# Attention scores of the first four stages read keys in place, and scale factors are finished on all partitions by one product each

## The chip, the cores and the metric

One core of a Trainium2 chip runs the whole program. The metric is the device time of one execution in microseconds (us); lower is better. Engines: PE is the matrix engine (PEld its weight loads), DVE the vector engine, ACT the activation engine, POOL the general engine, SP the queue that issues the DMAs.

## The reference, cut to what matters

```python
# q, k, v: (4, 8, 768, 64) float32; w_in (512, 2048), w_out (2048, 512) float64
k_sum = k.reshape(B, H, 24, 32, D).max(axis=3)       # one key for each block of 32
v_sum = v.reshape(B, H, 24, 32, D).mean(axis=3)
scores_l = scale * q @ k^T, kept where |i - j| < 16   # a band of 31 keys
scores_s = scale * q @ k_sum^T + log(32)              # 24 block keys
a = softmax(concat[scores_l, scores_s])               # minus row max; / (sum + 1e-9)
x = (a @ concat[v, v_sum]) with heads side by side    # (3072, 512)
h = x @ w_in;  out = (h * sigmoid(h)) @ w_out
```

## The kernel before, in words

The 3072 tokens are cut into 24 stages of 128 tokens (six for each of the four batches) and the feed-forward part into 12 chunks of 256 tokens, two stages each. A stage scores its 128 queries against a window of 158 keys and against the 24 block keys, so a score tile is 128x182. The first chunks need stages 0 to 3 before any feed-forward product can run.

Stages 0 to 5 (batch 0) multiply in float32; the first `NPL` = 4 stages are "plain" all through. Stages of later batches use pairs of float16, for which q, k and v are divided by power-of-two scales found from the data. A stage's steps and their lines in the kernel before:

- `job_k` (L365, L366): keys of a batch are loaded as four tiles (one for each pair of heads, 128x768) and DVE takes the maximum of each block into `km`. For batch 0 these tiles lie in space (`wt`) that holds weights later, and are free after the maximum.
- `job_qk` (L480, L492 to L497): for batch 0, `qkT` brings each pair of heads' 128 queries and 158 window keys in one DMA of 128x286, sixteen of them for stages 0 to 3; the 24 block keys are copied behind them by ACT or POOL (L214, L216).
- `job_mean` (L506, L523 to L528): six float32 products with `blocks` give the block means of v in bank 6, and DVE the largest |v|.
- `job_a` (L591 to L637): one score step on PE holds two pairs of heads, four products 64x128 by 64x182, the two heads of a pair on the upper and lower 64 rows of the array. DVE adds the mask and takes the maximum (L599), ACT the exponential (L602). In plain stages PE turns the result (L611, L613), and ACT or DVE copies it out.
- `job_c`, `job_x` (L657, L691, L695 to L697): PE multiplies by v and spreads 1/sum, DVE scales (L695), ACT rounds to `xh`, POOL or DVE takes the rest `xl`.
- `job_w` (L716 to L744): each of 16 weight tiles (1 MB) is loaded, changed from float64 bits to float32 by ACT and DVE, and scaled by a maximum over all partitions (L740).
- `job_f` (L801, L810): the two feed-forward products. ffn1 of a chunk and a tile f is two runs of 12 products, each 128x256; ffn2 is 12 products of 128x512.
- scales: `job_scale` (q and k), `v_scale` and `job_wo` (weights out). A column of 128 maxima is turned by PE into one row (L384, L425, L760), DVE works on that one partition (for q and k L388 to L394, seven short steps), PE spreads the results with a product with `ones` (L398, L437, L771), and DVE copies them out (L400, L438, L772).

The order on every engine is worked out when the program is built: a planner (`Plan`) takes the jobs with listed costs and priorities, assigns each to an engine, and writes each engine's queue. The priorities come from the table `TUNE`. Where it sees PE waiting at the start, it puts in idle products (L324, 128x256 bf16, result unused) to keep the clock up; it stops with them when the first feed-forward products stand.

Of the kernel before, what the change touches and what calls it, by code (L numbers as in the profile page):

```python
# [21 lines left out]
P = 128  # L22
# [185 lines left out]
def local_attn_ffn(ctx: ExitStack, tc: tile.TileContext, qkT, qF, qD, kF, kD, v, vR, w, out):  # L208
# [41 lines left out]
    ones = const.tile([1, P], F32, name="ones")  # L250
    nc.vector.memset(ones, 1.0)
# [15 lines left out]
    sc3 = const.tile([1, 4], F32, name="sc3")  # L267
# [29 lines left out]
    qc = const.tile([1, 10], F32, name="qc")  # L297
# [5 lines left out]
    sc2 = const.tile([1, 4], F32, name="sc2")  # L303
# [53 lines left out]

    def job_k(b, prio):
# [12 lines left out]
    def job_scale(b, prio):  # L371
# [9 lines left out]

        def tr(e, k=k):
# [3 lines left out]
        plan.op({"pe": 220}, tr, r=["qm_q", "qm_k"], w=[("bank", k)], prio=prio, cols=256)  # L386
        steps = (
            lambda e, k=k: nc.vector.tensor_reduce(out=qc[:, 0:2], in_=bank[k][:1, :2 * P].rearrange("o (a p) -> o a p", a=2), axis=AX.X, op=ALU.max),  # L388
# [3 lines left out]
            lambda e: nc.vector.reciprocal(out=qc[:, 6:8], in_=qc[:, 4:6]),  # L392
            lambda e: nc.vector.scalar_tensor_tensor(out=qc[:, 8:9], in0=qc[:, 4:5], scalar=-ISQ, in1=qc[:, 5:6], op0=ALU.mult, op1=ALU.mult),
            lambda e: nc.vector.scalar_tensor_tensor(out=qc[:, 9:10], in0=qc[:, 6:7], scalar=math.log(BLK) / ISQ, in1=qc[:, 7:8], op0=ALU.mult, op1=ALU.mult))  # L394
        for i, step in enumerate(steps):
            plan.op({"dve": 330 if i == 0 else 70}, step, r=[("bank", k)] if i == 0 else [], w=["qc"], prio=prio)
        k = sbank()
        plan.op({"pe": 110}, lambda e, k=k: nc.tensor.matmul(out=bank[k][:, :4], lhsT=ones, rhs=qc[:, 6:10], start=True, stop=True), r=["qc"], w=[("bank", k)], prio=prio, cols=1)  # L398
        qs = qsc_t[b % 2]
        plan.op({"dve": 67}, lambda e, k=k: nc.vector.tensor_copy(out=qs, in_=bank[k][:, :4]), r=[("bank", k)], w=[("qsc", b % 2)], prio=prio)  # L400
# [22 lines left out]
    def v_scale(b, prio):  # L423
        k = sbank()
        plan.op({"pe": 110}, lambda e, k=k: nc.tensor.transpose(out=bank[k][:1, :P], in_=am_t[:, 7:8], identity=ident), r=["am4"], w=[("bank", k)], prio=prio, cols=128)  # L425

        steps = (
            lambda e, k=k: nc.vector.tensor_reduce(out=sc2[:, 0:1], in_=bank[k][:1, :P], axis=AX.X, op=ALU.max),
# [3 lines left out]
            lambda e: nc.vector.reciprocal(out=sc2[:, 2:3], in_=sc2[:, 1:2]),  # L432
            lambda e: nc.vector.tensor_scalar(out=sc2[:, 3:4], in0=sc2[:, 1:2], scalar1=0.25, scalar2=None, op0=ALU.mult))
        for i, step in enumerate(steps):
            plan.op({"dve": 198 if i == 0 else 70}, step, r=[("bank", k)] if i == 0 else [], w=["sc2"], prio=prio)
        k = sbank()
# [540 lines left out]
```

## Time and profile before

| | |
|---|---|
| median of 3 runs | 631.01 us (630.73 to 631.74) |
| the profiled execution | 631.93 us, of which span 630.1 us |
| PE busy | 614.5 us (98%), 5008 products |
| DVE, ACT, POOL busy | 470.2, 397.2, 186.0 us |
| moved by DMA | 94.77 MB, mean 150 GB/s |

A row of the timeline gives start, duration, engine, line, operation, and in brackets how long the engine was idle before it and what ended that. Products are pipelined: a product's duration is its latency, and what a run of them costs is read from the distance between starts.

### The profile page before, as it was taken

Reading aid. Unit: us, or ns where it says so; the run is one execution under the profiler, and the core shown is the slowest. Engines: PE = TensorE matmul, PEld = TensorE weight load, DVE = VectorE, ACT = ScalarE, POOL = GpSimd, SP = SyncE. Lnnn points to the kernel's source line nnn. Section 1 sums busy time; section 2 is a strip of 40 time slices with the busy share of each in tenths; the row PEclk is TensorE's granted clock in tenths of the full one; section 3 lists DMA queues with packets and bytes.
Section 4 is the critical chain, followed back from the end, with each engine's and each line's share of the span. In section 5 each row is a group of like instructions: output and inputs, shape, how many; then the busy total and the mean of one; then the engine's idle time right before and its main releaser. Section 6 shows DMA issues by size and latency. Waiting matters only on the chain. (4 is left out here: it accounts for less than half of the span.)

```text
span 630.1 us, 13616 instructions
## 1 busy us (share of the span) xinstructions
PE 614.5 (98%) x5008; PEld 422.3 (67%) x5008; DVE 470.2 (75%) x1317; ACT 397.2 (63%) x860; POOL 186.0 (30%) x213
## 2 busy tenths in 40 slices
PE   7999999999999998999999998999999999999997
PEld 3877666666666765767767765766767767767674
DVE  7899877999797857898888864699888884562322
ACT  2899998764787666566676564565775673452322
POOL 3010531322734523325443253133343323110000
PEclk8999999999999999999999999999999999999999
DMA  9994755346574994454764774457566740220000
GB/s 300 363 377 196 277 171 167 85 135 182 152 173 121 205 232 151 121 152 111 155 176 111 205 203 125 122 147 158 165 153 122 208 101 14 59 39 14 34 1 33
DMA packets 92566, 94.77 MB, mean 150 GB/s; under 512 B 70460, under 2 KB 73532, under 8 KB 90452
## 3 DMA queue, kind: packets, MB, share of 16 engines
q1 hardware_dynamic: 92500, 93.91, 54.1%
q8 instruction: 39, 0.64, 0.5%
q14 instruction: 27, 0.22, 0.1%
HBM read 69.41 MB, written 6.29 MB: 120 GB/s over the span
## 5 line engine op out<-in xcount | busy, mean ns | idle before, releaser
L810 PE MATMUL bank<-wt,g 128*128 128x512 f16 (+1 forms) x1120 | 276.9, 392 | 4.7 <-POOL g L232 3.2
L801 PE MATMUL bank<-xh,wt 128*128 128x256 f16 x1536 | 269.8, 273 | 1.0 <-DVE raw L835 0.9
L801 PEld LDWEIGHTS <-wt 128*128 128x128 f16 x2304 | 224.3, 98 | 46.5 <-issue 6.5
L801 PE MATMUL bank<-xl,wt 128*128 128x256 f16 x768 | 209.3, 273 | 1.4 <-DVE xl L229 1.4
L810 PEld LDWEIGHTS <-g 128*128 128x128 f16 x1056 | 100.6, 98 | 107.5 <-POOL g L232 6.7
L816 DVE SCALAR_TENSOR_TENSOR t<-t,bank 128x512 f32<-128x512 f32 x96 | 65.5, 682 | 70.5 <-ACT t L815 70.2
L232 POOL TENSOR_TENSOR g<-t,g 128x512 f16<-128x512 f32 x56 | 72.4, 1292 | 152.6 <-ACT g L820 134.4
L815 ACT ACTIVATE t<-bank,asc 128x512 f32<-128x512 f32 x96 | 65.4, 681 | 81.8 <-PE bank L801 81.7
L602 ACT ACTIVATE e<-e,mx 128x182 f32<-128x182 f32 x192 | 83.6, 437 | 21.9 <-DVE mx L599 21.2
L637 DVE SCALAR_TENSOR_TENSOR p<-e,sum,p 128x128 f16<-128x128 f32 x320 | 89.7, 343 | 3.3 <-ACT p L624 2.4
L820 ACT CAST g<-t 128x512 f16<-128x512 f32 x88 | 54.0, 614 | 34.0 <-DVE t L816 33.5
L599 DVE CUSTOM_DVE_ANT_0 e<-bank,masks,qsc 128x182 f32<-128x182 f32 x144 | 52.1, 401 | 8.4 <-PE bank L594 8.1
L626 POOL TENSOR_SCALAR p<-e,sum 128x182 f16<-128x182 f32 x62 | 28.6, 470 | 99.4 <-ACT e L602 36.2
L624 ACT ACTIVATE p<-e,sum 128x182 f16<-128x182 f32 x75 | 30.3, 439 | 22.7 <-DVE sum L619 8.5
L232 POOL TENSOR_TENSOR vv<-raw,vv 128x1024 f16<-128x1024 f32 x17 | 37.5, 2206 | 14.8 <-ACT vv L214 10.9
L232 DVE TENSOR_TENSOR g<-t,g 128x512 f16<-128x512 f32 x32 | 31.1, 973 | 13.9 <-ACT g L820 12.8
L602 ACT ACTIVATION_READ_ACCUMULATOR e<-e,mx 128x1 f32 x192 | 36.0, 188 | 0.0
L497 DVE SCALAR_TENSOR_TENSOR qk<-raw,qsc,qk 64x1264 f16<-64x1264 f32 x18 | 28.9, 1608 | 5.9 <-ACT qk L496 3.8
L496 ACT ACTIVATE qk<-raw,qsc 128x1264 f16<-128x1264 f32 x18 | 24.2, 1345 | 11.7 <-DMA raw<-in_kD_dram 11.5
L593 PE MATMUL bank<-qk 128*128 128x182 f16 x144 | 27.8, 242 | 0.0
L594 PE MATMUL bank<-qk 128*128 128x182 f16 x144 | 27.8, 242 | 0.0
L670 PE MATMUL bank<-tt,vv 128*64 128x128 f16 x800 | 26.1, 220 | 0.0
(153 smaller groups left out, 632.0 us busy)
## 6 DMA issues: line engine op xcount, KB each, us to landing
wt<-in_w_dram SPq DMA_DIRECT2D x16, 1024.0 KB
raw<-in_kD_dram SPq DMA_DIRECT2D x18, 632.0 KB
raw<-in_v_dram SPq DMA_DIRECT2D x20, 512.0 KB
raw<-in_qD_dram SPq DMA_DIRECT2D x18, 512.0 KB
out_dram<-raw SPq DMA_DIRECT2D x24, 256.0 KB
raw<-in_kF_dram SPq DMA_DIRECT2D x12, 384.0 KB
raw<-in_qF_dram SPq DMA_DIRECT2D x9, 512.0 KB
raw<-in_vR_dram SPq DMA_DIRECT2D x12, 384.0 KB
```

What stands on the lines that cost most here:

```text
L232: eng[e].tensor_tensor(out=out, in0=in0, in1=in1, op=ALU.subtract)
L497: plan.op({"dve": 1450}, lambda e: nc.vector.scalar_tensor_tensor(out=kst[64:, :, :NLOC], in0=kr[64:], scalar=qs[64:, 1:2], in1=kst[64:, : ...
L599: plan.op({"dve": 258 if b == 0 else 323}, lambda e, i=i: nc.vector.tensor_tensor_reduce(out=et[:, i, :NKEY], in0=sc[:, i, :NKEY], in1=mas ...
L602: plan.op({"act": 431}, lambda e, i=i, h=h: nc.scalar.activation(out=et[:, i, :NKEY], in_=et[:, i, :NKEY], func=AF.Exp, scale=-1.0, bias=m ...
L624: nc.scalar.activation(out=out, in_=et[:, i, :NKEY], func=AF.Copy, scale=by)
L626: nc.gpsimd.tensor_scalar(out=out, in0=et[:, i, :NKEY], scalar1=by, scalar2=0.0, op0=ALU.mult, op1=ALU.add)
L637: nc.vector.scalar_tensor_tensor(out=pt[:, i, to:to + z - a], in0=et[:, i, a:z], scalar=su[:, i:i + 1], in1=pt[:, i, a:z], op0=ALU.mult, o ...
L801: nc.tensor.matmul(out=h[:, d * CH:(d + 1) * CH], lhsT=wt[f, 0][:, part, d, ct * P:(ct + 1) * P], rhs=x[:, ct, :], start=(ct == 0 and q == ...
L810: nc.tensor.matmul(out=bank[ob[u]], lhsT=a[:, d * CH + u * P:d * CH + u * P + P], rhs=b[:, d, :], start=(opens and d == 0 and q == 0), sto ...
L815: plan.op({"act": 640}, lambda e: nc.scalar.activation(out=t, in_=h, func=AF.Tanh, scale=asc_t[c // 3 % 2][:, f:f + 1]), r=[("bank", k), ( ...
L816: plan.op({"dve": 605}, lambda e: nc.vector.scalar_tensor_tensor(out=t, in0=t, scalar=1.0, in1=h, op0=ALU.add, op1=ALU.mult), r=[("bank", ...
L820: plan.op({"act": 540}, lambda e: nc.scalar.copy(out=gh, in_=t), r=[("t", j)], w=[("gh", n)], prio=at - TUNE["post"])
```

## The change

Plain stages no longer load windows of keys. Their scores read the keys from the four tiles that `job_k` loads, with zeros of 15 columns on each side (POOL, eight memsets), and the block keys from `km`: a score step has eight products (158 and 24 columns) in place of four (182). The window is contiguous (15 before to 15 after), so these stages have a mask of their own (`band`), rows of v in another order, and left operands of the block means to match (`blocks0`, `blocks1`). Only the queries are loaded, two DMAs of 128x256 for each of the four stages. The key tiles stay in use until the scores of stage 3. The 24-column copies now serve stages 4 and 5.

Scales: one float32 product of the column, spread over 128 columns, with the identity puts all 128 values on every partition. DVE does the same short steps on 128 partitions and writes the last into their place; the second product and the copy are gone. `TUNE` is changed.

```diff
@@ job_k
+            if b == 0:
+                plain_k[hp] = stg[:, :S + 2 * HALO], key
+                kf = stg[:, HALO:HALO + S]
+                for side in (stg[:, :HALO], stg[:, HALO + S:S + 2 * HALO]):
+                    nc.gpsimd.memset(side, 0.0)
@@ job_scale (v_scale and job_wo alike)
-                nc.tensor.transpose(out=bank[k][:1, j * P:(j + 1) * P], in_=qm_t[:, 3 + 5 * j:4 + 5 * j], identity=ident)
+                nc.tensor.matmul(out=bank[k][:, j * P:(j + 1) * P], lhsT=qm_t[:, 3 + 5 * j:4 + 5 * j].to_broadcast([P, P]), rhs=ident, start=True, stop=True)
...
-        plan.op({"pe": 110}, lambda e, k=k: nc.tensor.matmul(out=bank[k][:, :4], lhsT=ones, rhs=qc[:, 6:10], start=True, stop=True), ...)
-        plan.op({"dve": 67}, lambda e, k=k: nc.vector.tensor_copy(out=qs, in_=bank[k][:, :4]), ...)
@@ job_qk
+        if s < NPL:
+            qk = qk_t[s % 2].bitcast(F32)[:, :4 * P].rearrange("p (a n) -> p a n", a=4)
+            for hp in range(0, 4, 2):
+                plan.op({"dma": 460}, lambda e, hp=hp: nc.sync.dma_start(out=qk[:, hp:hp + 2], in_=q0[t, :, hp:hp + 2]), ...)
+            return
@@ job_a
-        mask = masks[:, 0 if t == 0 else (2 if t == NTILE - 1 else 1), :]
+        mask = band[:, 0 if t == 0 else 1, :] if s < NPL else masks[:, 2 if t == NTILE - 1 else 0 if t == 0 else 1, :]
...
+                        if plain:
+                            at = i * 256
+                            for rhs in (plain_k[hp][0][pr, t * P:t * P + NLOC], km_t[0][pr, hp, :]):
+                                to = at + rhs.shape[-1]
+                                nc.tensor.matmul(out=bank[k + o][:, at:to], lhsT=qk[pr, hp, :], rhs=rhs, start=True, stop=True)
+                                at = to
+                            continue
```

On PE, the first products after the idle ones. `wt_76` and `wt_77` hold v, `wt_68` and `wt_69` keys, `qk0` the first stage's queries (before: with keys). Before:

```order
L525 MATMUL bank6_205<-wt_76,blocks_105 24x512
L525 MATMUL bank6_205<-wt_77,blocks_105 24x512
...
L591 MATMUL bank2_201<-qk0_151 128x182
L591 MATMUL bank3_202<-qk0_151 128x182
...
L525 MATMUL bank6_205<-wt_71,blocks_105 24x512
```

After:

```order
L619 MATMUL bank2_224<-wt_69,qk0_174 128x158
L619 MATMUL bank2_224<-km0_182,qk0_174 128x24
L619 MATMUL bank3_225<-wt_69,qk0_174 128x158
L619 MATMUL bank3_225<-km0_182,qk0_174 128x24
...
L549 MATMUL bank6_228<-wt_76,blocks0_114 24x512
L549 MATMUL bank6_228<-wt_77,blocks1_109 24x512
```

The first score step has moved ahead of the block means of v, four of which stood before it. Up to the first feed-forward product there stood five score steps, nine turned banks (four products each), two spreads of 1/sum and 61 idle products; now there stand seven, twelve, three and 48.

On SP, the loads around the weights of tile f = 2 (`wt_68` and `wt_69`) and f = 3 (`wt_70` and `wt_71`), with what each waits for (DMAHW are the DMA queues' own). Before:

```order
L716 DMA wt_64<-in_w_dram 128x2048 [waits DMAHW2_49]
...
L716 DMA wt_66<-in_w_dram 128x2048 [waits DMAHW7_49]
L716 DMA wt_65<-in_w_dram 128x2048 [waits DMAHW0_49]
...
L716 DMA wt_68<-in_w_dram 128x2048 [waits DMAHW3_49,DVE_49]
...
L716 DMA wt_70<-in_w_dram 128x2048 [waits DMAHW6_49,DVE_49]
```

After:

```order
L753 DMA wt_67<-in_w_dram 128x2048 [waits DMAHW7_49]
...
L753 DMA wt_72<-in_w_dram 128x2048 [waits DMAHW2_49]
L753 DMA wt_73<-in_w_dram 128x2048 [waits DMAHW3_49]
...
L753 DMA wt_74<-in_w_dram 128x2048 [waits DMAHW5_49]
L753 DMA wt_68<-in_w_dram 128x2048 [waits DVE_49,DMAHW6_49,PE_49,Pool_49]
...
L753 DMA wt_70<-in_w_dram 128x2048 [waits DVE_49,DMAHW1_49,PE_49,Pool_49]
```

The loads of `wt_68` and `wt_70` have moved from fourth and fifth of the weight loads to eighth and ninth, and wait for PE too, whose last reader of those tiles is stage 3's scores.

On PE, the scale of q and k for batch 1, near 127 us of the profile before: the second product stands between two halves of an ffn2. Before:

```order
L810 MATMUL bank4_203<-wt_79,g2_198 128x512
L398 MATMUL bank6_205<-qc_156,ones_85 128x4
L810 LDWEIGHTS g2_198
L810 MATMUL bank5_204<-wt_79,g2_198 128x512
...
L591 MATMUL bank6_205<-qk1_152 128x182
```

After, the only product of that scale stands inside an ffn1:

```order
L835 MATMUL bank1_223<-xh1_214,wt_78 128x256
L409 MATMUL bank6_228<-ident_80,qm_178 128x128 x2
L835 LDWEIGHTS wt_78
L835 MATMUL bank1_223<-xh1_214,wt_78 128x256
L835 LDWEIGHTS wt_78
```

The visit that waited for the seven DVE steps is gone; what is left takes the place of L384.

More of the change, by code (lines that the diff above doesn't have):

```diff
@@ L391, in job_scale @@
             lambda e: nc.vector.tensor_scalar(out=qc[:, 4:6], in0=qc[:, 2:4], scalar1=2.0 ** -14, scalar2=None, op0=ALU.mult),
-            lambda e: nc.vector.reciprocal(out=qc[:, 6:8], in_=qc[:, 4:6]),
-            lambda e: nc.vector.scalar_tensor_tensor(out=qc[:, 8:9], in0=qc[:, 4:5], scalar=-ISQ, in1=qc[:, 5:6], op0=ALU.mult, op1=ALU.mult),
-            lambda e: nc.vector.scalar_tensor_tensor(out=qc[:, 9:10], in0=qc[:, 6:7], scalar=math.log(BLK) / ISQ, in1=qc[:, 7:8], op0=ALU.mult, op1=ALU.mult))
+            lambda e: nc.vector.reciprocal(out=qs[:, 0:2], in_=qc[:, 4:6]),
+            lambda e: nc.vector.scalar_tensor_tensor(out=qs[:, 2:3], in0=qc[:, 4:5], scalar=-ISQ, in1=qc[:, 5:6], op0=ALU.mult, op1=ALU.mult),
+            lambda e: nc.vector.scalar_tensor_tensor(out=qs[:, 3:4], in0=qs[:, 0:1], scalar=math.log(BLK) / ISQ, in1=qs[:, 1:2], op0=ALU.mult, op1=ALU.mult))
         for i, step in enumerate(steps):
[L396 to L400, printed above, removed]
+            plan.op({"dve": 330 if i == 0 else 70}, step, r=[("bank", k)] if i == 0 else [], w=["qc"] + ([("qsc", b % 2)] if i > 3 else []), prio=prio)
     def job_km(b, prio):
@@ L475, in job_qk @@
         b, t = divmod(s, NTILE)
+        if s < NPL:
+            qk = qk_t[s % 2].bitcast(F32)[:, :4 * P].rearrange("p (a n) -> p a n", a=4)
+            for hp in range(0, 4, 2):
+                plan.op({"dma": 460}, lambda e, hp=hp: nc.sync.dma_start(out=qk[:, hp:hp + 2], in_=q0[t, :, hp:hp + 2]), w=[("qk", s % 2, hp + i) for i in range(2)], prio=prio + hp // 2)
+            return
         if b == 0:
@@ L524, in job_mean @@
             at = (NTILE - 1 - t) * 4
-            plan.op({"pe": 1020}, lambda e, src=src, t=t, at=at, k=k: nc.tensor.matmul(out=bank[k][:NB], lhsT=blocks[:, at:at + NB], rhs=src, start=(t == 0), stop=(t == NTILE - 1)),
+            of = blocks0 if t == 0 else (blocks1 if t < NPL else blocks)[:, at:at + NB]
+            plan.op({"pe": 1020}, lambda e, src=src, t=t, of=of, k=k: nc.tensor.matmul(out=bank[k][:NB], lhsT=of, rhs=src, start=(t == 0), stop=(t == NTILE - 1)),
                     r=key, w=[("bank", k)], prio=prio, cols=2048)
@@ L596, in job_a @@
         if b or g % 2 == 0:
-            plan.op({"pe": 330 if b else 820}, scores, r=[(x, s % 2, hp) for x in ("qk", "qkm") for hp, _ in heads(g)] + [("qkk", s % 2)], w=[("bank", k)] if b else [("bank", k), ("bank", k + 1)], prio=prio, cols=728)
+            need = [("qk", s % 2, hp) for hp, _ in heads(g)] + [("qkk", s % 2)]
+            if plain:
+                need += [(x, s % 2, hp) for x in ("qk", "qkm") for hp in range(4) if (x, s % 2, hp) not in need]
+                need += [x for hp, _ in heads(g) for x in [("km", hp)] + plain_k[hp][1]]
+            else:
+                need += [("qkm", s % 2, hp) for hp, _ in heads(g)]
+            plan.op({"pe": 330 if b else 950 if plain else 820}, scores, r=need, w=[("bank", k)] if b else [("bank", k), ("bank", k + 1)], prio=prio, cols=728)
         for i, (hp, h) in enumerate(heads(g)):
@@ L853, in job_stage @@
         if s == 0:
-            plan.op({"pool": 1}, lambda e: None, w=["mask"] + [("qkk", i) for i in range(2)], prio=-90.0)
+            plan.op({"pool": 1}, lambda e: None, w=["mask"] + [("qkk", i) for i in range(2)] + [("qkm", i, hp) for i in range(2) for hp in range(4)], prio=-90.0)
             job_k(0, -74)
@@ L904, in local_attn_ffn @@
     plan.issue()
[L907 removed]
+TUNE = dict(wo=1725.55, kap=515.89, km=254.54, w_dma=-435.28, w_dec=16.19, a0=529.03, a1=-254.77, d1=354.23, span=-231.56, post=-299.98, ffn2=-1403.83, jc0=2185.03, jc1=787.71, jx0=754.54, jx1=-298.86, vs=2845.05, qk=-522.95, k=325.28, v=1913.04, v0=-151.46, out=847.66, first=347.6)
 NUDGE = {}
[L913 removed]
+_INS = ["q0", "qkT", "qF", "qD", "kF", "kD", "v", "vR", "w"]
 def _layout(inputs):
```

77 lines of the change are left out of this document (47 added, 30 removed).

## The prediction

> **What bounds the kernel now.** I read the page first, then the time by stretches, then the timeline of the first 46 us, then the waits of PE.
>
> ```profile
> PE 614.5 (98%) x5008; PEld 422.3 (67%) x5008; DVE 470.2 (75%) x1317; ACT 397.2 (63%) x860; POOL 186.0 (30%) x213
> PEclk8999999999999999999999999999999999999999
> L324 PE MATMUL bank<-ident 128*128 128x256 bf16 x61 | 9.4, 305 | 1.4 <-POOL ident masks.py:199 1.4
> ```
>
> PE is busy for 614.5 of 630.1 us, so 15.6 us are idle, and part of the busy time is the 61 idle products. What is to be had are those, the idle time, and products that can be left out. Where they lie, in stretches (length, busy time of PE, PEld, DVE, ACT and POOL with counts, granted clock, DMA share, GB/s):
>
> ```profile
> 0.00:5.00 5.00, 3.64 (x20) 2.60 (x20) 3.56 (x20) 1.28 (x1) 3.20 (x17) 1.00 0.63 203
> 5.00:10.00 5.00, 2.81 (x5) 0.57 (x5) 4.97 (x9) 0.64 (x3) 1.78 (x5) 0.76 1.04 359
> 10.00:15.00 5.00, 5.00 (x19) 1.52 (x18) 2.77 (x11) 1.28 (x6) 0.21 (x1) 0.90 1.10 327
> 15.00:20.00 5.00, 5.00 (x41) 3.48 (x40) 3.96 (x21) 3.94 (x16) 0.00 (x0) 1.00 0.80 259
> 30.00:35.00 5.00, 4.95 (x51) 4.01 (x48) 5.00 (x13) 5.00 (x11) 2.46 (x2) 1.00 1.01 400
> 125.00:150.00 25.00, 22.74 (x185) 14.38 (x184) 24.23 (x66) 13.64 (x34) 4.82 (x7) 1.00 0.56 154
> 225.00:250.00 25.00, 22.64 (x190) 15.45 (x189) 14.62 (x31) 13.41 (x25) 7.26 (x6) 1.00 0.71 197
> 375.00:400.00 25.00, 22.99 (x193) 15.63 (x192) 12.82 (x28) 12.79 (x22) 6.39 (x4) 1.00 0.47 138
> ```
>
> Two kinds of place: the first 15 us, where PE, DVE and ACT wait for data and PE loses 3.6 us, and three spots of about 2 us where a new batch comes in. At 30 to 35 us DVE and ACT are full. The timeline shows what starts the work:
>
> ```profile
> 5.38 2.60 DVE L366 TENSOR_REDUCE km<-wt 128x24 f32<-128x768 f32 x3
> 7.29 5.29 PE L525 MATMUL bank<-wt,blocks 128*24 128x512 f32 x8 [2.19 <-DMA wt<-in_v_dram]
> 11.21 0.95 DVE L366 TENSOR_REDUCE km<-wt 128x24 f32<-128x768 f32 x1 [0.86 <-DMA wt<-in_kF_dram]
> 12.51 0.89 PE L591 MATMUL bank<-qk 64*128 64x182 f32 x8
> 13.33 0.50 PE L324 MATMUL bank<-ident 128*128 128x256 bf16 x3
> 13.54 0.35 DVE L599 CUSTOM_DVE_ANT_0 e<-bank,masks 128x182 f32<-128x182 f32 x1 [1.38 <-PE bank L591]
> 22.76 1.09 PE L691 MATMUL bank<-ident,ss 128*64 128x128 f32 x16
> 23.58 0.91 PEld L657 LDWEIGHTS bank<-wt 128*64 128x64 f32 x16
> 30.54 0.89 PE L591 MATMUL bank<-qk 64*128 64x182 f32 x8
> 31.36 3.01 PE L324 MATMUL bank<-ident 128*128 128x256 bf16 x26
> 31.76 0.68 DVE L695 TENSOR_TENSOR xr<-bank,xr 128x512 f32<-128x512 f32 x1
> 34.78 0.29 PEld L611 LDWEIGHTS bank<-ident,e 128*128 128x128 f32 x2
> 35.25 1.30 PEld L801 LDWEIGHTS <-wt 128*128 128x128 f16 x12
> ```
>
> The first mask step waits for the first score step, which stands behind four block means. The first feed-forward product starts at 35.25; the second scaling (L695) that its input needs ends at 32.44. Two costs are read here from distances: a score step is 0.82 us (30.54 to 31.36), a spread of 1/sum 0.82 (22.76 to 23.58), a turned bank 0.47 (34.78 to 35.25), an idle product 0.11 to 0.12 (3.06 us for 26).
>
> **The change part by part.**
>
> Start of the first scores. The step needs two key tiles, their maxima and the first queries, no longer four block means and a late copy. DVE's three maxima start at 5.38, 0.87 us each, right behind its setup. The change adds eight short setup steps there, about 0.6 us by the length of the ones shown (fills of 128x474: 0.45), so they come at 6.0, the second is done at 7.7. The score step then runs when the clock was halved before (0.76 in 5 to 10 us), so I double it to 1 to 2 us; the planner has put one |v| maximum ahead on DVE. First mask step at about 9.6 in place of 13.54: 3.9 us earlier. POOL's extra masks and the zero columns, fourteen steps, end before 8 by its rows of 0.1 to 0.3 us.
>
> What DVE then does up to the second scaling. Counted in the order, the changed kernel has 8 more mask steps (0.27 apart), 3 more |v| maxima, one more key maximum, one weight maximum and one xr scaling more, and two copies and the vsc copy less:
>
> ```profile
> 7.90 2.45 DVE L528 TENSOR_REDUCE am<-wt 128x1 f32<-128x512 f32 x4
> 24.98 1.20 DVE L736 TENSOR_REDUCE wm<-wt 128x1 f32<-128x1024 f32 x1
> 28.76 0.75 DVE L226 TENSOR_SCALAR xr<-bank,vsc 128x512 f32<-128x512 f32 x1 [0.57 <-PE bank L691]
> 27.50 0.63 DVE L218 COPY wt<-bank 128x512 f32<-128x512 f32 x1
> 22.12 0.14 DVE L438 COPY vsc<-bank 128x2 f32<-128x2 f32 x1
> ```
>
> 2.2 + 1.8 + 0.9 + 1.2 + 0.75 - 1.3 - 0.1 = 5.4 us. The second scaling ends at 32.4 - 3.9 + 5.4 = 33.9, 1.5 us later than before. PE's own list up to the same point, from 7.7: seven score steps, six means (0.86 each, half of 1.9 for four rows at the full clock being 0.95), twelve banks at 0.47, three spreads at 0.82, two products with v at 2.0, small ones 0.5, 27 idle ones at 0.11: 8.2 + 5.2 + 5.6 + 2.5 + 4.0 + 0.5 + 3.0 = 29.0, so 36.7, or 37.7 with the slow clock. I take the first feed-forward product at 37.2, 2.0 us later. By then PE has done more: two score steps, three banks and one spread, 1.64 + 1.41 + 0.82 = 3.9 us. Net 1.9 us gained, provided PE stays full afterwards, which the stretches after 35 us allow.
>
> A split score step. It has 16 records in place of 8. Per half of the array before: four streams of 0.15 us (0.61 in all, the loads' row below). After: four of 158/182 of that, and four short ones that cost no less than a weight load. A 128-column float32 load is 0.11 us by the spread's row (0.29 for two with a tail of 0.18). If both halves run side by side as now: 4 x 0.13 + 4 x 0.11 = 0.97, so 0.35 more. Bounds: nothing (hidden loads), or 16 loads one after another, 1.75 in place of 0.82, so 0.93 more. I take 0.35, since the row shows eight loads in 0.61. Seven of eight steps are in the list above (at 1.17 each); the last costs 0.35.
>
> ```profile
> 21.95 0.61 PEld L591 LDWEIGHTS bank<-qk 64*128 64x128 f32 x8 [0.21 <-issue]
> 21.31 0.29 PEld L437 LDWEIGHTS bank<-sc,ones 1*128 1x128 f32 x2 [0.37 <-DVE sc L433]
> 21.62 0.39 PE L324 MATMUL bank<-ident 128*128 128x256 bf16 x2
> ```
>
> [...]
>
> Scales. After 35 us ten transposes (0.11 each, one record) become products of two records (0.22 by the turned bank's two), 1.1 us more; seven second products go, 0.31 each (21.31 to 21.62), 2.2 us less: 1.1 us gained on PE, as PE is full. DVE's short steps on 128 partitions in place of one I cost at nothing: a two-element step of 128 partitions (L438) took 0.14 us, as those on one did; a maximum over 128x128 in place of 1x128 the same. Bounds: 0 to 0.1 us for each chain, off PE's path. With the second product goes PE's wait for the chain:
>
> ```profile
> 126.93 0.38 PE L398 MATMUL bank<-qc,ones 1*128 1x4 f32 x2 [0.98 <-DVE qc L394]
> 127.60 1.16 POOL L232 TENSOR_TENSOR g<-t,g 128x512 f16<-128x512 f32 x1 [3.92 <-DVE qsc L400]
> PE bank L810 <- POOL g L232: 3.2, 5, 1.0
> ```
>
> 0.98 us were lost there; behind it stood half an ffn2. I take 0.5 of it, between 0 and 0.98, because the next PE waits are for POOL's g (3.2 us in five places), which the chain does not shorten. The other waits of that kind I leave as they are: the whole order is new, and they may come out either way by about 3 us.
>
> Loads. Stages 0 to 3 bring 0.26 MB in place of 0.59 each: 1.3 MB, at 400 GB/s 3.3 us of a queue that is full in the first 45 us. I give no time for it: the weights of f = 0 and 1 come earlier, and DVE, ACT and PE, not they, end the start. Eight DMA issues fewer on SP.
>
> Sum: -1.9 + 0.35 - 1.1 - 0.5 = -3.2 us. The profiled execution took 631.93 (630.1 of span and 1.8 around it) and would take 628.7; it lies 0.9 above the median 631.01, so the median goes to 627.8.
>
> **The rivals.**
>
> More than that: the waits at the batches' borders go as well. They are 2.3, 2.4 and 2.0 us in the three stretches above; if half of them go, 624.5. For it: the chains are shorter there. Against it: most of that idle time ends with POOL's g, not a scale.
>
> No change: weights of f = 2 and 3 come late. Their tiles hold the keys until stage 3's scores, and the loads stand on SP behind that wait, with all later loads behind them. In the trace a 1 MB load takes 2.6 us at 400 GB/s, plus about 2 to start, and the steps after it (L724, L726, L736, L222, L229 by their rows 6.0, with the maximum over partitions) some 6.6:
>
> ```profile
> 28.78 1.13 ACT L222 ACTIVATE wt<-wt,ur 128x1024 f16<-128x1024 f32 x1
> 30.56 1.28 DVE L229 SCALAR_TENSOR_TENSOR wt<-wt,ur 128x1024 f16<-128x1024 f32 x1
> 31.39 1.16 ACT L724 ACTIVATE wt<-wt 128x1024 f32<-128x1024 f32 x1
> 29.43 1.22 DVE L726 SCALAR_TENSOR_TENSOR wt<-wt 128x1024 uint32<-128x1024 uint32 x1
> ```
>
> With stage 3's first scores done at 37, f = 2 could be ready at 48, and PE's list reaches it some 17 to 19 us after its first ffn1, at 55; for f = 3 there are some 6 us. If queues on the full DVE and ACT eat more than these 6 to 7 us, PE waits; 3 us of it gives 631.
>
> Slower: the split step runs its loads one after another, 1.75 us each. Seven steps before the first ffn1 then cost 4.1 us more than I took, the last 0.6: 627.8 + 4.7 = 632.5. It decides from about 1.6 us a step on.
>
> Little changes at all: DVE, not PE, sets the start, and later starts eat the gain. That gives the same 631 as the late weights.
>
> **How the numbers follow.** A measurement of this kernel can tell 0.2%, 1.3 us, from no change: faster is below 629.7, slower above 632.3. My forecast (627.8, its own range 626.0 to 629.6) 0.46; more than that (624.5) 0.17; no change (631) 0.22; slower (632.5 and above) 0.15. So faster 0.63, same 0.22, slower 0.15. The range from 624.6 to 632.3 leaves out the tails of the first and last rivals, about 0.2.
>
> **What would show it.** The first mask step near 9.6 us and the first ffn1 near 37; 16 loads of a score step in 1.0 us and not 1.7; no wait of PE on a scale's DVE steps; idle products 48; weights of f = 2 ready before PE reaches them, that is no PE wait on a weight's DVE or ACT step at 45 to 65 us. Wrong would be a first ffn1 after 40, a second half-clock stretch (each is 3.4 us by the 0.76 and 0.90 above, and costs up to 1.7), or more than 9 us of PE idle time after 100 us.

## The result, and the profile after

The change makes the kernel slower: 639.28 us (median of 4 runs, 636.7 to 640.5) against 630.9 (now median of 4 runs of the kernel before, 630.73 to 631.74), a ratio of 1.0121 with a 95% interval of 1.0082 to 1.0160. I had said 627.8, so the sign was wrong and the time off by 11.5 us. The profiled execution took 640.47, its span is 638.6.

First the page of the kernel after, then the same stretches of time as before (length, busy time of PE, PEld, DVE, ACT and POOL with counts, granted clock, DMA share, GB/s):

```profile
PE 618.1 (97%) x5054; PEld 425.6 (67%) x5054; DVE 477.6 (75%) x1310; ACT 397.2 (62%) x871; POOL 190.5 (30%) x222
```

```profile
5.00:10.00 5.00, 2.96 (x20) 1.99 (x18) 4.73 (x9) 0.00 (x0) 3.50 (x19) 0.92 1.01 368
10.00:15.00 5.00, 5.00 (x12) 1.46 (x11) 4.43 (x14) 1.83 (x8) 0.00 (x0) 0.50 1.05 393
15.00:20.00 5.00, 5.00 (x38) 2.61 (x39) 1.62 (x9) 2.40 (x8) 0.00 (x0) 0.90 0.35 82
125.00:150.00 25.00, 23.63 (x200) 15.78 (x198) 24.34 (x65) 13.97 (x34) 4.55 (x6) 1.00 0.58 149
225.00:250.00 25.00, 22.35 (x221) 15.56 (x221) 19.06 (x59) 17.57 (x47) 10.38 (x11) 1.00 0.72 184
375.00:400.00 25.00, 24.07 (x201) 16.26 (x199) 18.43 (x58) 12.85 (x32) 4.99 (x7) 1.00 0.49 111
```

The clock column now has 0.92, 0.50 and 0.90 where before had 0.76 and 0.90. In steps of 0.5 us the column falls to 0.50 and no lower in both traces (8.0 to 11.0 us before, 9.5 to 16.0 after). So the time at half clock is twice what is missing to 1: 2 x 5 x (0.08 + 0.50 + 0.10) = 6.8 us, and before 2 x 5 x (0.24 + 0.10) = 3.4 us. In the three later stretches, where PE lost 2.3, 2.4 and 2.0 us before, it now loses 1.4, 2.7 and 0.9, so what is new lies elsewhere. From 15 to 20 us PE counts as busy all through, yet DVE and ACT, at 3.96 and 3.94 there before, have 1.62 and 2.40, and the DMA queue, at 0.80 before, 0.35. The timeline of PE and DVE shows what they wait for:

```profile
2.39 0.17 DVE L279 COPY blocks<-blocks 128x4 f32<-128x4 f32 x1 [0.53 <-POOL blocks L276]
3.79 0.07 DVE L288 MEMSET band<- 128x15 f32 x1 [0.80 <-POOL band L287]
7.52 2.61 DVE L389 TENSOR_REDUCE km<-wt 128x24 f32<-128x768 f32 x3
...
10.64 0.34 DVE L636 CUSTOM_DVE_ANT_0 e<-bank,band 128x182 f32<-128x182 f32 x1
...
18.38 0.35 DVE L636 CUSTOM_DVE_ANT_0 e<-bank,band 128x182 f32<-128x182 f32 x1 [3.95 <-PE bank L619]
```

```profile
7.02 0.53 PE L619 MATMUL bank<-wt,qk 64*128 64x158 f32 x2 [1.02 <-POOL wt L387]
8.47 0.29 PE L619 MATMUL bank<-km,qk 64*128 64x24 f32 x1 [0.92 <-DVE km L389]
...
10.41 3.61 PE L549 MATMUL bank<-wt,blocks 128*24 128x512 f32 x4
13.95 0.69 PE L648 MATMUL bank<-ident,e 128*128 128x128 f32 x2
...
17.04 0.55 PE L619 MATMUL bank<-wt,qk 64*128 64x158 f32 x4
17.41 0.31 PE L619 MATMUL bank<-km,qk 64*128 64x24 f32 x4
...
18.16 1.04 PE L549 MATMUL bank<-wt,blocks 128*24 128x512 f32 x2
```

DVE's setup waits twice for POOL's new masks, so the key maxima start at 7.52, not at the 6.0 that I had taken. PE's first score product waits for POOL's zeros beside the keys (1.02), then for `km` (0.92). The first mask step still comes early, at 10.64. But then block means and turns run at half the clock from 10.41 to 16, the second score step stands behind them on PE until 17.04, and DVE waits 3.95 us for it. PE itself has no listed wait from there to the first feed-forward product. Its waits up to 45 us (engine, tile and line that waits, what it waits for, us in total, times, longest):

```profile
PE bank L340 <- POOL ident masks.py:199: 1.4, 1, 1.4
PE bank L619 <- POOL wt L387: 1.0, 1, 1.0
PE bank L619 <- DVE km L389: 0.9, 1, 0.9
```

So the start lasts as long as PE's own list. On SP two pairs of loads take 7.59 and 13.32 us to issue, and the next loads there follow only at 18.64 and 43.95 (the first pair is stage 2's queries, waiting for stage 0's scores, the second weights, waiting for the keys' tiles):

```profile
11.00 7.59 SPq L497 DMA_DIRECT2D qk<-in_q_dram  x2
...
30.58 13.32 SPq L753 DMA_DIRECT2D wt<-in_w_dram  x2
```

The second scaling (L732 after, L695 before) follows late, and ahead of the first feed-forward product now stand one more spread of 1/sum, idle products and a score step (L619):

```profile
39.15 0.68 DVE L732 TENSOR_TENSOR xr<-bank,xr 128x512 f32<-128x512 f32 x1
```

```profile
40.30 1.09 PE L728 MATMUL bank<-ident,ss 128*64 128x128 f32 x16
41.32 1.05 PE L340 MATMUL bank<-ident 128*128 128x256 bf16 x8
42.30 0.57 PE L619 MATMUL bank<-wt,qk 64*128 64x158 f32 x4
...
43.43 0.28 PE L835 MATMUL bank<-xh,wt 128*128 128x256 f16 x1
```

Before, it stood here:

```profile
35.36 0.27 PE L801 MATMUL bank<-xh,wt 128*128 128x256 f16 x1
```

So the first feed-forward product is at 43.43 in place of 35.36, 8.1 us later, with 3.9 us more work done by then (as the prediction counted it): 4.2 us lost. The rest is PE's idle time behind the start, from 20 to 620 us, first before, then after:

```profile
20.00:620.00 600.00, 591.63 (x4900) 411.36 (x4899) 453.54 (x1257) 387.43 (x833) 180.85 (x191) 1.00 0.54 148
```

```profile
20.00:620.00 600.00, 586.66 (x4885) 408.05 (x4882) 461.10 (x1253) 387.56 (x850) 184.17 (x190) 1.00 0.54 146
```

8.4 us idle before, 13.3 after, 5.0 more. 4.2 + 5.0 less some 1 us that the scales save is near the 8.5 us between the two spans. Which waits these are, from 45 us on:

```profile
PE bank L844 <- POOL g L232: 2.6, 5, 0.7
PE bank L624 <- DVE mx L636: 2.3, 2, 1.6
PE bank L409 <- DVE qm L401: 1.8, 1, 1.8
PE bank L476 <- DVE vm L468: 1.3, 1, 1.3
PE bank L648 <- ACT e L639: 1.2, 1, 1.2
PE bank L707 <- DMA tt<-p: 1.2, 1, 1.2
...
PE bank L624 <- DVE qc L413: 0.9, 1, 0.9
```

The wait of L398 for the scale's short steps (0.98) is gone with its product, but the first scores of a batch (L624) now wait 0.9 us for those steps. And the new order put the first product of a scale (L409) where its input, the sum over q, is not there yet, and the turned sums of v (L476) likewise, and first scores whose bank DVE has not yet read (L624): 1.8 + 1.3 + 2.3 us. Before, of these three, the list has only the turned sums, with 0.2 us:

```profile
PE bank L458 <- DVE vm L450: 0.2, 1, 0.2
```

Weights are not in the list of the kernel after.

### The profile page after: what moved, and what is told of

Read it like the earlier page. It is cut to its first block, busy times and chain, and to the rows that moved or that the text cites. A ratio compares the mean times of both kernels' runs of the same rounds, so it can differ in the third digit from the quotient of the medians.

```text
span 638.6 us, 13705 instructions
## 1 busy us (share of the span) xinstructions
PE 618.1 (97%) x5054; PEld 425.6 (67%) x5054; DVE 477.6 (75%) x1310; ACT 397.2 (62%) x871; POOL 190.5 (30%) x222
## 5 line engine op out<-in xcount | busy, mean ns | idle before, releaser
L232 POOL TENSOR_TENSOR g<-t,g 128x512 f16<-128x512 f32 x58 | 75.5, 1301 | 153.1 <-ACT g L854 144.0
L639 ACT ACTIVATE e<-e,mx 128x182 f32<-128x182 f32 x192 | 83.6, 438 | 42.5 <-DVE mx L636 41.7
L674 DVE SCALAR_TENSOR_TENSOR p<-e,sum,p 128x128 f16<-128x128 f32 x320 | 101.3, 379 | 6.0 <-ACT p L661 3.9
L663 POOL TENSOR_SCALAR p<-e,sum 128x182 f16<-128x182 f32 x55 | 25.6, 470 | 76.4 <-DVE sum L656 37.6
L661 ACT ACTIVATE p<-e,sum 128x182 f16<-128x182 f32 x79 | 31.6, 437 | 19.2 <-issue 8.9
L232 POOL TENSOR_TENSOR vv<-raw,vv 128x1024 f16<-128x1024 f32 x17 | 38.9, 2288 | 5.9 <-ACT vv L214 3.8
L232 DVE TENSOR_TENSOR g<-t,g 128x512 f16<-128x512 f32 x30 | 24.0, 801 | 18.0 <-ACT g L854 17.8
L519 ACT ACTIVATE qk<-raw,qsc 128x1264 f16<-128x1264 f32 x18 | 24.2, 1342 | 10.4 <-DMA raw<-in_kD_dram 10.0
L624 PE MATMUL bank<-qk 128*128 128x182 f16 x144 | 27.3, 241 | 3.2 <-DVE mx L636 2.3
L655 DVE TENSOR_SCALAR sum<-sum 128x2 f32<-128x2 f32 x80 | 23.5, 306 | 7.2 <-ACT e L639 6.9
```

Source lines behind the costliest of these rows:

```text
L232: eng[e].tensor_tensor(out=out, in0=in0, in1=in1, op=ALU.subtract)
L624: nc.tensor.matmul(out=sc[:, i, :NKEY], lhsT=qh[:, h, :], rhs=kst[:, h, :], start=True, stop=False)
L639: plan.op({"act": 431}, lambda e, i=i, h=h: nc.scalar.activation(out=et[:, i, :NKEY], in_=et[:, i, :NKEY], func=AF.Exp, scale=-1.0, bias=m ...
L661: nc.scalar.activation(out=out, in_=et[:, i, :NKEY], func=AF.Copy, scale=by)
L674: nc.vector.scalar_tensor_tensor(out=pt[:, i, to:to + z - a], in0=et[:, i, a:z], scalar=su[:, i:i + 1], in1=pt[:, i, a:z], op0=ALU.mult, o ...
```

## The experiments

Ratios are to the kernel before on the same chip, with their 95% intervals. The last two columns are of one profiled execution each: when the first feed-forward product starts, and PE's idle time from 20 to 620 us (600 less PE's busy time in that stretch). They vary between executions, the first above all with how fast the first products run (see e6: 6.44 us for eight records of means, where the profile before has 5.29), so the ratios decide.

| | ratio | first ffn1 | PE idle |
|---|---|---|---|
| before | 1 | 35.4 | 8.4 |
| after | 1.0121 (1.0082 to 1.0160) | 43.4 | 13.3 |
| e1 more idle products, on after | 1.0073 (1.0051 to 1.0095) | 40.5 | 10.4 |
| e2 DVE setup later, on after | 1.0079 (1.0052 to 1.0106) | 40.4 | 12.1 |
| e5 both, on after | 1.0041 (1.0018 to 1.0064) | 39.3 | 9.8 |
| e12 e5, three PE steps later | 1.0113 (1.0084 to 1.0142) | 38.9 | 16.5 |
| e11 keys in own space, on after | 1.0126 (1.0086 to 1.0165) | 43.1 | 11.5 |
| e3 old numbers, on after | 1.0214 (1.0182 to 1.0246) | 41.7 | 10.6 |
| e4 new numbers, on before | 1.0215 (1.0196 to 1.0234) | 37.5 | 15.6 |
| e8 new scales, re-planned, on before | 1.0175 (1.0142 to 1.0209) | 41.0 | 13.1 |
| e6 new scales, old order | 0.9969 (0.9943 to 0.9996) | 37.2 | 6.9 |
| e7 split scores, old order | 1.0001 (0.9977 to 1.0025) | 35.3 | 5.9 |
| e9 whole change, old order | 0.9989 (0.9968 to 1.0009) | 36.4 | 5.7 |
| e10 e9, first score step ahead | 0.9981 (0.9960 to 1.0002) | 36.2 | 6.4 |
| e14 e10, more idle products | 0.9926 (0.9896 to 0.9955) | 35.2 | 5.6 |
| e13 e14, second score step ahead | 0.9958 (0.9932 to 0.9984) | 35.5 | 4.0 |
| e16 e13, DVE and third step freed | 0.9960 (0.9933 to 0.9988) | 36.7 | 5.6 |
| e15 before, more idle products | 0.9929 (0.9905 to 0.9953) | 34.0 | 6.4 |
| e17 e15 with the scales of e6 | 0.9912 (0.9884 to 0.9941) | 34.7 | 6.7 |

The theories: A, the start (clock, setup, second score step); B, the new order of the whole program; C, the split and in-place scores cost by themselves (the row groups in what was expected of e1 and e9 are the upper and lower 64 rows of PE, one for each head of a pair).

**The start: e1, e2, e5.** Idle products ahead of the first product of the plan, and three setup steps of DVE behind those that wait for nothing:

```diff
+        more = 25
+            if e == "pe":
+                fills, more = fills + more, 0
```

> Only change: 25 more idle products ahead of the first product of the plan; the planned order is the same. Theory A (the start: PE is too lightly loaded between 7 and 16 us, so the granted clock stays at half from 9.20 to 16.02 and the second score step comes 4 us late): the half-clock stretch after 10 us shrinks to at most 2 us, the fifth mask step comes by about 16 instead of 18.4, the first product with w1 at about 40 to 41 instead of 43.4, and the total falls by 2 to 4 us, to 635 to 637. Theory B (the order that the new numbers give loses its time at the batch borders after 100 us, and the late start is only moved slack): the start comes earlier, the total stays within 1 us of 639.3. Theory C (the split steps and the row-group loads cost it everywhere): no change of the start either.

```diff
-    nc.vector.tensor_copy(out=blocks0[:, :4], in_=blocks1[:, 20:24])
-    nc.vector.memset(blocks0[:HALO, HALO:HALO + 1], 1.0 / BLK)
-    nc.vector.memset(band[:, 0, :HALO], NEG)
...
     for i in range(2, 6):
         nc.vector.memset(bank[i], 0.0)
+    nc.vector.tensor_copy(out=blocks0[:, :4], in_=blocks1[:, 20:24])
+    nc.vector.memset(blocks0[:HALO, HALO:HALO + 1], 1.0 / BLK)
+    nc.vector.memset(band[:, 0, :HALO], NEG)
```

> Only change: the three setup steps of DVE that touch what POOL's masks write (the copy into blocks0 with its edge value, the edge of band) stand behind the setup steps that wait for nothing. Theory A: the first key maximum comes at 6.0 to 6.5 instead of 7.52 and the first mask step 0.5 to 1.2 earlier than 10.64; the total falls by 0.5 to 1.5 us. Theory B or C: the total stays within 0.7 us of 639.3. A rival within A: what sets the first score step is POOL's zeros beside the keys (done at 7.28), then the first mask step moves by less than 0.3.

e5 has both, with 14 idle products.

> The kernel after with both edits of the start: the three setup steps of DVE later, and 14 more idle products. If both act on the same loss (the half clock during the block means between the first and second score step), the total is that of either alone, 636 to 638, ratio about 1.007. If they act on different losses (the clock, and the late key maxima), it adds up: first product with w1 at 38.5 to 39.5, ratio about 1.003. Theory B (the order): no lower than the two.

e1: the half clock after 10 us is gone (granted clock 1.00 in 10 to 15 us), the fifth mask step is at 15.41, the first feed-forward product at 40.45, and the ratio falls by 0.0048, 3.0 us: theory A as written. With e2 the key maxima start at 6.00, and the ratio falls by 0.0042, more than the 1.5 us expected; but its interval overlaps that of the kernel after, so e2's gain by itself is not shown. Its profiled execution has 3.4 us at half clock in the first 20 us (0.80 and 0.86 in 5 to 15 us), and two more stretches of it later (mean clock 0.97 over 45 to 100 us and 0.98 over 200 to 300). Together the two edits take 0.0080, 5 us, off, clear of the intervals, and the first product with w1 comes at 39.3. That is two thirds of the loss, had back at the start (the controls below show that idle products give as much without the change). One third, 0.0041, is not, so A is not all of it.

**Keys in own space: e11.** Is it the weights that wait 13.32 us on SP?

```diff
+                stg = own_k[hp]
-                plain_k[hp] = stg[:, :S + 2 * HALO], key
+                plain_k[hp] = stg, key
```

> The kernel after, order kept, with the keys in the space of later turned tiles in place of weight tiles: the weights of f = 2 and 3 no longer wait for the scores of stage 3 on SP (13.32 us of it in the trace of after). Rival 'weights late': the total falls by 2 us or more, ratio 1.009 or below. Theory A and B: PE never waits for these weights, so the ratio stays at 1.011 to 1.013.

No: 1.0126, where the rival said 1.009 or below; and no weights stand in the list of PE's waits. My rival of late weights is out.

**The order: e3, e4, e8.** The numbers of `TUNE` (22 of them) exchanged both ways, and the new scales alone with the order worked out anew.

```diff
-TUNE = dict(wo=1725.55, kap=515.89, km=254.54, w_dma=-435.28, ...
+TUNE = dict(wo=1435.66, kap=595.44, km=324.46, w_dma=-292.18, ...
```

> The kernel after with the 21 planning numbers of the kernel before. Theory B: the planned order decides, and with the old numbers the time falls by 3 us or more, below 636. Theory A: the score steps without means and with split products are planned early with either set, the half-clock stretch stays, and the total is 637 to 643.

> The kernel before with the 21 planning numbers of the kernel after; nothing else of the change. Theory B: the numbers make the stalls at the batch borders, 634 to 637. Theory A: the new keys and setup at the start make the loss, so this kernel stays at 630 to 633.

> The same instructions as the kernel before with the new scales, but the order worked out anew from the new costs, with the old 21 numbers. Theory B (any new order loses time at the borders that the old order, found by trying numbers, does not): slower than the one with the order kept by 3 us or more. Theory A (the loss is in the start of the new keys): within 1.5 us of it.

Neither theory had this: each set of numbers is bad for the other program, by 0.9% (e3 against after) and 2.2% (e4 against before). So it was not the new numbers as such. Three more orders of nearly the same instructions come out 1.8 to 2.2% above before. e4 shows it plainest: not one instruction of the change, first ffn1 only 2.2 us late, and 15.6 us of idle time in place of 8.4.

The idle column does not hold all of it. In several profiled executions the clock was at half again behind the start, about 3.4 us at a time (0.97 over 45 to 100 us in e5 is 2 x 55 x 0.03 = 3.3): in e3 three times between 20 and 620 us, in e8 and e2 twice, in e1, e4, e5, e6 and e12 once, in the others not at all. PE counts as busy in it, and by an estimate, half of its 3.4 us, each time costs up to 1.7 us, in e3 up to 5.1 of the 9.5 us that its span is longer than before's. In e5 it follows a PE wait of 1.20 us for ACT: four ffn2 products then take 3.48 us from start to start (50.90 to 54.38), the next four 1.72 (54.82 to 56.54). In e12 it follows one of 3.99 us, near 145 us. Not every such wait has one behind it: the 1.7 us for `qm` in e5 and, in the kernel after, 1.8 for `qm` and 1.2 for ACT's `e` have none. So some waits of PE may cost time twice; no run tests that alone. In e12 the clock column has 0.78 and 0.88 (2 x 5 x (0.22 + 0.12) = 3.4 us):

```profile
145.00:150.00 5.00, 2.47 (x26) 1.65 (x26) 0.44 (x1) 1.15 (x1) 0.70 (x1) 0.78 0.85 287
150.00:155.00 5.00, 5.00 (x32) 3.16 (x31) 4.17 (x12) 2.86 (x5) 1.16 (x1) 0.88 0.09 20
```

**The order kept: e6, e7, e9.** The planner is fed the steps and costs of before, so that every engine's queue stays as it was. Where the change has no instruction, nothing is issued; where it has another, that one.

```diff
# e6
-        plan.op({"pe": 110}, lambda e, k=k: nc.tensor.matmul(out=bank[k][:, :4], lhsT=ones, rhs=qc[:, 6:10], start=True, stop=True), ...)
-        plan.op({"dve": 67}, lambda e, k=k: nc.vector.tensor_copy(out=qs, in_=bank[k][:, :4]), ...)
+        plan.op({"pe": 110}, lambda e: None, ...)
+        plan.op({"dve": 67}, lambda e: None, ...)
```

> The kernel before with the scales done in the new way and nothing else; the planned order is kept as it was, with nothing issued at the places of the second product and the copy. The prediction's terms for the scales: 1.1 us of PE and 0.5 us of a wait, so 1 to 1.6 us less than before, ratio about 0.998. Rival: the waits at the batch borders end with something else (POOL's g), and what PE saves is waited out there: ratio 0.9995 to 1.0005.

```diff
# e7
-                        nc.tensor.matmul(out=bank[k + o][:, i * 256:i * 256 + NKEY], lhsT=qk[pr, hp, :P], rhs=qk[pr, hp, P:], start=True, stop=True)
+                        for lo, hi in (((0, NLOC), (NLOC, NKEY)) if plain else ((0, NKEY),)):
+                            nc.tensor.matmul(out=bank[k + o][:, i * 256 + lo:i * 256 + hi], lhsT=qk[pr, hp, :P], rhs=qk[pr, hp, P + lo:P + hi], start=True, stop=True)
```

> The kernel before with each score product of stages 0 to 3 split into one of 158 and one of 24 columns, keys where they were; the planned order is kept. A split step costs 0.29 us more by the trace of after (1.11 in place of 0.82), eight of them 2.3. Of these, PE stands idle or in idle products behind five, so the total grows by 1 to 2.3 us, ratio 1.002 to 1.004. Rival (loads are hidden, or the steps lie beside DVE): within 0.5 us.

> Both halves of the change, with the order of the kernel before kept on every engine: the keys stay in space of their own (that of the turned tiles of later stages), so that no weight load waits for them; the scales as in e6; the three setup steps of DVE late. The 24-column copies of stages 4 and 5 go to POOL. Theory B (the loss of the change is the new order): not slower than e6, ratio 0.993 to 0.998. Theory C (reading keys in place costs by itself, by split steps and loads in row groups): ratio 0.999 to 1.004.

The scales alone give 0.9969, 2.0 us, and by the interval 0.3 to 3.6: the predicted 1.6 is inside, and the rival (no gain, 0.9995 and above) just touches the interval. e8 has the same arithmetic and lies 2.1% above it: that is the price of an order. The profile of e6 also shows how far one execution's start can differ. Its clock column has 1.00 over the first 15 us, yet the first eight records of means take 6.44 us, where they took 5.29 in the profile before and 3.59 in e15's:

```profile
7.90 6.44 PE L526 MATMUL bank<-wt,blocks 128*24 128x512 f32 x8 [2.10 <-DMA wt<-in_v_dram]
```

So in this profile a 1.00 at the start stands beside slow products, and their speed is read from their own records; and e6's first feed-forward product, at 37.2, is late for these slow products and for v, which came 0.6 us later, not for the scales. The split alone gives 1.0001, not the 1.002 to 1.004 expected. Its 0.30 us a step (below) may lie beside other work; no run shows that, and the interval allows 1.6 us either way. The whole change in the old order is 0.9989 (in e9 batch 0's block keys have a tile of their own too). Theory B had said not above e6 and at most 0.998, and theory C 0.999 and above, so the median lies with C by a hair: if reading keys in place costs anything by itself, it is about 0.2% against e6, inside both intervals, and the scales pay for it. PE's idle time there is 5.7 us:

```profile
20.00:620.00 600.00, 594.26 (x4958) 416.64 (x4957) 455.07 (x1258) 388.96 (x839) 183.40 (x199) 1.00 0.53 147
```

So the change as a whole, in the old order, costs nothing that can be measured. e9 differs from the kernel after in two more things, the keys' own space (worth nothing in e11) and the setup steps of e2 (up to 0.4%); a pair without that difference is e5 and e14, below.

**What the rest of the order's loss is: e12.** On e5, the three PE steps with the longest waits for one input each were moved, with what depends on them, behind the next one or two feed-forward runs.

```diff
+LATER = (("turn14", 1), ("vm1", 2), ("scale2", 2))
```

> As e5 (the new order with both edits of the start), and three steps of PE with what hangs on them moved behind the next one or two feed-forward runs: a turn of stage 3 that waits 1.20 us for ACT at 50 us, the turned sums of v that wait 1.32 us for DVE at 145 us, and the scale product of batch 2 that waits 1.72 us for the sum of q at 250 us. If the rest of the loss is such steps placed too early by the plan, the ratio falls from 1.0041 by 0.003 to 0.006, to about 1.000. Rival: the wait comes back at the next step that needs the same data (scores of the new batch), or DVE is late throughout; then it falls by less than 0.002.

The rival won, and by more than it had said: 1.0113, 4.5 us worse than e5. The waits of e5 and, behind, those of e12:

```profile
PE bank L412 <- DVE qm L404: 1.7, 1, 1.7
PE bank L847 <- POOL g L235: 1.7, 4, 0.7
PE bank L479 <- DVE vm L471: 1.3, 1, 1.3
PE bank L651 <- ACT e L642: 1.2, 1, 1.2
```

```profile
PE bank L732 <- DMA tt<-p: 4.4, 2, 4.0
PE bank L869 <- POOL g L257: 3.1, 7, 0.7
PE bank L649 <- DVE qc L438: 2.5, 2, 2.0
PE bank L869 <- ACT g L247: 2.1, 1, 2.1
```

The three waits are gone (4.2 us), and 4.0 us for a turned tile by DMA, 2.0 for the scale's short steps (L438) and 2.1 for ACT's g have come in their place; behind the 4.0 us wait stands the half clock shown above. Here the steps that PE waited for were also ones that others waited for: moving them later saved the wait at that place and lengthened the chain behind it.

**What the early scores are worth: e10, e13 to e16.** In e10 three steps of the old order are moved ahead: the first queries' load, the first score step, its masks.

```diff
+        move("q0", ahead="v")
+        move("score0", ahead="mean")
+        move("mask0", behind=self.tags["score0"][0])
```

> As e9, and three moves alone: the first queries' load ahead of v on SP, the first score step ahead of the block means on PE, its four mask steps ahead of three |v| maxima on DVE. This is the start that the prediction hoped for, in an order that is otherwise that of before. If the early first step brings what the prediction said, the first mask step is at 8.5 to 10, the first product with w1 1 to 2 us earlier than in e9, and the ratio 0.002 to 0.003 lower. Rival: the second step, behind the block means, sets the start, and the ratio is that of e9 within 0.001.

The mask step moved from 14.14 (e9) to 9.48, the first feed-forward product by 0.3, the ratio by 0.0008. The rival's figure came: 4.7 us earlier at the first mask step bring no gain that can be measured there. The two intervals leave room for some 2.4 us. e13 added idle products and moved the second score step, e14 the idle products alone, e16 went further than e13; e15 is the control, before and 20 idle products.

```diff
# e13
+        move("exp0", behind=self.tags["mask0"][-1])
+        move("turn0", ahead="mean4")
+        move("score2", ahead="mean4")
+        line = [o[:4] + (o[4] + 22,) if o[2] == self.tags["score0"][0] else o for o in line]
# e16, besides
+        move("mask3", behind=self.tags["mask2"][-1])
+        move("score4", ahead="vs0")
```

> As e10 (the order of before, first score step and its masks ahead), and: 22 more idle products ahead of it, so that the clock is not halved; the turns of the first step and the second score step ahead of the last two block means. The eighth mask step then comes at 15 to 16.5 instead of 19.34, and the first product with w1 1.5 to 3 us earlier than 36.17. If the early scores are worth what the prediction said (1.9 us), the ratio is 0.994 to 0.997. Rival: DVE and ACT, full from 25 us on, set the first product with w1; then it moves less than 0.7 us and the ratio stays at 0.998.

> e10 and 22 more idle products ahead of the first score step, nothing else. If the clock is what keeps the early scores from paying: first product with w1 at about 35.5 as in e13, ratio 0.995 to 0.997. If the second score step behind the block means is: it stays at 36 and the ratio at 0.998 (e10), and the difference to e13 is the second step's.

> The kernel before and 20 more idle products ahead of its first block means, nothing of the change. If what e13 gained over e9 (0.003) is only the clock, this gains as much, ratio 0.996 to 0.998. If it is the early scores, this stays at 0.999 to 1.001.

> e13, and the two steps that still stood in the way there: the third score step on PE ahead of the scale product of v, and the second two mask steps of the second score step on DVE ahead of the scale's short steps, for which DVE stood idle 2.38 us. If the chain of scores sets the start: first product with w1 1 to 2 us earlier than 35.48, ratio 0.992 to 0.995. Rival: what is full from 25 us on (ACT and DVE with the weights) sets it, and nothing changes, 0.995 to 0.997.

e13 by itself looked like the gain that I had predicted. The control says otherwise: idle products alone, with nothing of the change, give 0.9929, and e14 with the change 0.9926. e13 and e16, with more of the scores early, are no better (0.9958 and 0.9960, the intervals overlap): in e13 the eighth mask step came at 18.55, not at 15 to 16.5, since DVE stood behind the scale's steps; in e16 it came at 16.33, and the first feed-forward product still went from 35.48 to 36.72. So early first scores bring nothing measurable; the idle products do. PE's list says why the first can be: in before, e9 and e10 PE has no listed wait from its first product of the plan to 36 us, so moving a score step ahead on PE does not shorten what PE has to do. In e15 the clock is full where before had 0.76 and 0.90, and the first eight records of means take 3.59 us where they took 5.29:

```profile
5.00:10.00 5.00, 4.70 (x28) 2.40 (x26) 4.97 (x9) 0.63 (x3) 1.76 (x5) 1.00 1.02 349
10.00:15.00 5.00, 5.00 (x25) 1.94 (x24) 3.83 (x14) 2.31 (x10) 0.21 (x1) 1.00 1.07 327
```

```profile
1.36 5.94 PE L326 MATMUL bank<-ident 128*128 128x256 bf16 x40 [1.36 <-POOL ident masks.py:199]
7.61 3.59 PE L527 MATMUL bank<-wt,blocks 128*24 128x512 f32 x8 [0.30 <-DMA wt<-in_v_dram]
```

The control also corrects e1 and e5: idle products are worth about as much to before as to after. With idle products and late setup steps in both, the new order (e5, 1.0041) is still 1.1% above the old (e14, 0.9926), clear of both intervals. That is the loss that goes with the order.

**A version that beats both: e17.** The new scales in the old order, with 20 more idle products.

```diff
+            if fills > 10 and e == "pe" and not seen_fill:
+                seen_fill, fills = True, fills + 20
```

> The kernel before with the new scales in the old order (e6) and 20 more idle products ahead of its first block means (e15). If the two gains are independent (0.0031 and 0.0071), the ratio is 0.988 to 0.992. If the scales' gain was only chance or lies beside what the clock changes, it is that of e15, 0.992 to 0.995.

626.64 us, ratio 0.9912: inside the range of two independent gains, but its interval takes in e15's 0.9929 too, so that the scales add to it is possible and not shown.

## Why the prediction was wrong, point by point

- The start, "net 1.9 us gained": 4.2 us lost. This is the term that failed most, by 6.1 us. The step that failed is the sum of PE's list: 29.0 us from 7.7 us on, and measured 36.4 from 7.02, with no listed wait behind 8.47. By the distances between starts (number of steps in brackets):

| us of PE up to the first ffn1 | predicted | before | after |
|---|---|---|---|
| score steps | 8.2 (7) | 4.1 (5) | 10.1 (7) |
| block means | 5.2 (6) | 7.1 (6) | 7.9 (6) |
| turned banks | 5.6 (12) | 4.7 (9) | 6.6 (12) |
| spreads of 1/sum | 2.5 (3) | 1.9 (2) | 3.1 (3) |
| products with v, small ones | 4.5 | 5.3 | 5.3 |
| idle products | 3.0 (27) | 5.0 (41) | 3.4 (27) |
| sum | 29.0 | 28.1 | 36.4 |

The first score step took 3.4 us for the 1.17 listed (7.02 to 10.41), 0.9 of it a listed wait for `km`. That wait comes from DVE: its new setup was counted by its length (0.6 us) and not by its waits for POOL (0.53 + 0.80), so the maxima came at 7.52 and not at 6.0, where e2 has them. The half clock was put on the first score step alone, with up to 1 us; it lasted 6.8 us, over the block means and turns, which costs up to 3.4 (an estimate, half of it), and without it (e1) the first ffn1 came 3.0 us earlier. A mean at full clock is 0.96 us (18.16 to 19.12), near the 0.95 of the working, and not the 0.86 in the sum. DVE's list (all lengths, no waits) missed its 3.95 us behind the second score step, so the second scaling ended at 39.83 and not at 33.9.

- The price put on it: 3.9 us earlier at the first mask step counted as 3.9 us earlier at the end of the chain. In e10 4.7 us of it moved the first ffn1 by 0.3, as PE's list, which has no listed wait there, set the end.
- "The other waits of that kind I leave as they are; they may come out either way by about 3 us": they came out 5.0 us the bad way. This is the error in kind: the order of the whole program was new, and I priced that at zero on the mean without a reason. Four orders made by the same planner for nearly the same work (after, e3, e4, e8) lie 1.2 to 2.2% above before; none lies below. Three of the four go by numbers set for another program; the kernel after goes by its own and still loses. With the start's edits on both sides the price is 1.1%, some 7 us (e5 against e14). The case "the new order itself costs" was no rival and had no chance of its own, which is also why the range ended at 632.3.
- A split score step: 1.17 us predicted, 1.12 measured (17.04 to 18.16), against 0.82. Its effect on the total is not measurable (e7). The upper bound, 16 loads of 0.11 one after another, was 0.93 more; measured was 0.30 more, with each short product on the same 64 rows as the one ahead of it. Which loads ran beside which products no run separates.
- Scales, -1.1 - 0.5: e6 has -2.0 (-3.6 to -0.3). The size agrees, though the interval nearly reaches zero. The DVE chain on 128 partitions cost little, as taken: a maximum over 128x128 took 0.28 us (L449 after) and one over 1x128 0.27 (L428 before), over 256 columns 0.42 (L413) and 0.40 (L388).
- The rival of late weights had its wait in the trace (13.32 us on SP), and no price (e11). The rival of serial loads is out by the 1.12. The rival that DVE and not PE sets the start had it the wrong way round: DVE delayed PE's first score step by 0.9 us, and then waited 3.95 us for PE.
- Of what I named as signs of a wrong prediction all three came: a first ffn1 after 40, a second half-clock stretch, more than 9 us of PE idle time after 100 us (12.0, for 8.2 before).

What stays open: why the four new orders have 2 to 7 us more idle time behind the start. Part of the price of such waits may be the half clock seen behind some of them (e5, e12); why the orders have the waits is not known. e12 shows that moving the three steps with the longest waits on PE does not mend it; whether it is DVE's or the DMA queue's order there was not tried. And e15's 4.5 us is more than the 1.7 us estimated for one half-clock stretch. In its profile, 3.5 us shorter, 1.3 us come at the first feed-forward product and 2.0 as less idle time later (6.4 for 8.4), so the earlier start may be passed on at the borders, which was not tested alone. Idle time also differs by 2 us between executions of kernels that are near alike (e9, e10, e13, e14 and e16 have 4.0 to 6.4), so these two figures may be chance.

## What to carry to other kernels

Where a program's order is worked out by a planner, a change of the code is two changes: keep the old order (feed the planner the old steps and issue the new instructions in their places) before judging the edit. Price a new order as a cost of its own, from other orders of the same program, and not as zero. And run a control with each helper alone: the idle products that seemed to rescue the change were worth as much without it.

## What was not expected of the hardware

Twenty idle products, put where PE waits for its first data anyway, make a kernel of 630 us 0.7% faster (e15). In its profile the granted clock is 1.00 through the first 15 us and the first eight records of means take 3.59 us in place of 5.29, which can be up to 1.7 of the 4.5 us; the rest is not explained. And the clock fell to half not only at the start: in eight of the profiled executions it did so in the middle of the program, for about 3.4 us at a time, in e5 behind a PE wait of 1.20 us and in e12 behind one of 3.99. In e5 four ffn2 products took 3.48 us in it and the next four 1.72, so this stretch cost some 1.8 us on top of the wait.
